# A layer-norm pipeline staggered by half tiles, w1 in column quarters, and segment sums moved from TensorE to VectorE

## The chip, the cores and the metric

The kernel runs on one core of one Trainium2 chip. The time is device microseconds (us) of that core for one execution. A difference of under 2% in either direction is called "same", with a 95% interval beside it.

Engine names in the profile: PE is the TensorE matmul, PEld its weight load, DVE is VectorE, ACT is ScalarE, POOL is GpSimd, SP is SyncE, which here only issues DMAs. "SPq" is SyncE's own queue of DMA issues. L401 is line 401 of the kernel that the profile belongs to, so the same statement has another number in another kernel.

## The reference, cut to what matters

```python
x  = A_x                                   # 2048 tokens x 1024, bf16
xn = layernorm(x)
return x + A(xn, mem0, Wq, Wk, Wv, Wo) + B(xn, w1, w2, w3, w4)

def B(x, w1, w2, w3, w4):
    h  = gelu(layernorm(x) @ w1)           # 1024 -> 1024
    hs = shift_four_column_groups(h) @ w2  # tokens moved by +1, -1, +2, -2
    x1 = x + hs
    return x1 + gelu(layernorm(x1) @ w3) @ w4     # 1024 -> 3584 -> 1024

def A(x, mem, ...):                        # 64 segments of 32 tokens, 8 memory tokens
    for s in range(64):                    # 32 heads of 128
        h = concat(mem, x[segment s])
        o = attention(h) @ Wo              # memory tokens see all 40, the others none later than themselves
        mem = o[:8]; outs.append(o[8:])
```

The kernel runs B first and fits work for A between its matmuls. The part of A that matters here starts from the sums of `xn` over each segment of 32 tokens. They are multiplied by Wv ("vb" units: 32 matmuls each), then by Wo ("g" units), then by Wv again ("vr" units), to get values for the memory tokens before the attention begins. There are eight units of each kind, in that order.

## The kernel before

Comments in the code are added here. The order of stages is: stage 1 (layer-norms, transposes, w1, gelu), stage 2 (w2, residual, second layer-norm), four passes of 512 tokens each through w3 and then w4, the V stage, the attention, and the output projection. A tile is 128 tokens. `NPE` is the number of tiles that are normalised on VectorE and transposed by TensorE; the later ones are normalised on ScalarE and transposed by DMA.

```python
NPE = 8
load_x(0)
load_x(1)
for c in range(2):                                       # w1 in two column halves
    nc.sync.dma_start(w1_sb[:, :, c * 512:(c + 1) * 512], w1_v[:, :, c * 512:(c + 1) * 512])
    load_x(c + 2)
# ... cut
def norm2(n, xn2T, jj):
    if n < NPE:
        nc.vector.tensor_scalar(xn2[:], xts[n][:], mv[:, 0:1], rr[:, 1:2], op0=ALU.subtract, op1=ALU.mult)
    else:
        nc.scalar.activation(xn2[:], xts[n][:], ACTF.Identity, bias=nm2[:], scale=rr[:, 1:2])
        nc.sync.dma_start_transpose(xn2T[:, jj], xn2[:])

def seg_sums(n, xn):                                     # in stage 1, from SBUF
    ps = psum0.tile([P, KT, 4], F32, tag="xs")
    for k in range(KT):
        nc.tensor.matmul(ps[:, k, :], xn[:, k * P:(k + 1) * P], segsum[:], start=True, stop=True)
    nc.scalar.copy(xsum[:, :, 4 * n:4 * n + 4], ps[:])
# ... cut: stage 1 and stage 2
for _ in range(4):
    load_w3()
for c in range(7):                                       # w4, 7 x 1 MB, on the SP queue
    nc.sync.dma_start(w4_sb[:, 4 * c:4 * (c + 1), :], w4_v[:, 4 * c:4 * (c + 1), :])

def unit_vb(hg):
    wv = wtile()
    nc.gpsimd.dma_start(wv[:], Wv_v[:, :, hg * 512:(hg + 1) * 512])
    def run():
        ps = psum3.tile([P, 4, NQ], F32, tag="vr")       # NQ = 71 columns
        for hh in range(4):
            for k in range(KT):
                nc.tensor.matmul(ps[:, hh, :], wv[:, k, hh * P:(hh + 1) * P], xb[:, k, :NQ], start=(k == 0), stop=(k == KT - 1))
        # ... cut
def load_r1(n):                                          # the residual of tile n, two buffers
    nc.sync.dma_start(r1s[n][0][:], R1_v[:, n, :])
    nc.sync.dma_start(r1s[n][1][:], x_v[:, n, :])

load_r1(0)
for tb in range(4):                                      # the four passes
    depth = 1 if tb < 2 else 2
    for f in range(FT):                                  # w3, FT = 28
        # ... cut: 8 matmuls and a gelu
        if tb == 0 and f == 20:
            mem_start()                                  # copies xsum and the memory's sum to xb
        if tb > 0 and f % 7 == 6:
            spec_step(depth)                             # runs one vb, g or vr unit, loads the next
    if tb == 0:
        spec_load()
    for j in range(4):                                   # w4, one tile at a time
        n = tb * 4 + j
        R1, xt = r1s.pop(n)
        load_r1(n + 1)
        nc.gpsimd.tensor_tensor(R1[:], R1[:], xt[:], op=ALU.add)
        # ... cut: 2 x 28 matmuls, two adds to R1 on VectorE
        if n == NT - 1:
            while pending or units:
                spec_step(depth)
        elif n > 0:
            spec_step(depth)
```

Of the kernel before, what the change touches and what calls it, by code (L numbers as in the profile page):

```python
# [77 lines left out]
def kernel(  # L78
# [47 lines left out]
    segsum_np = np.zeros((P, 4), np.float32)  # L126
    for t in range(P):
        segsum_np[t, t // SEG] = 1.0
    segsum = const_tile("c_segsum", segsum_np)
# [54 lines left out]
    with tc.manual_schedule(engines={mybir.EngineType.PE, mybir.EngineType.SP, mybir.EngineType.Pool}), ExitStack() as actx:  # L184
# [6 lines left out]
        with ExitStack() as bctx:  # L191
            w3ctx = bctx.enter_context(ExitStack())
            xctx = bctx.enter_context(ExitStack())
            xsum = xctx.enter_context(tc.tile_pool(name="xs", bufs=1)).tile([P, KT, NSEG], BF16)
# [12 lines left out]
            with ExitStack() as hctx:  # L207
# [7 lines left out]
                with ExitStack() as p0:  # L215
# [3 lines left out]
                    NPE = 8  # L219
# [9 lines left out]
                    load_x(1)  # L229
                    for c in range(2):  # L230
                        nc.sync.dma_start(w1_sb[:, :, c * 512:(c + 1) * 512], w1_v[:, :, c * 512:(c + 1) * 512])
                        load_x(c + 2)
                    for n in range(4, 7):
                        load_x(n)
# [54 lines left out]
                    def seg_sums(n, xn):  # L289
                        ps = psum0.tile([P, KT, 4], F32, tag="xs")  # L290
                        for k in range(KT):
                            nc.tensor.matmul(ps[:, k, :], xn[:, k * P:(k + 1) * P], segsum[:], start=True, stop=True)  # L292
                        nc.scalar.copy(xsum[:, :, 4 * n:4 * n + 4], ps[:])

                    def stage1(n0, nt, xn2T, between):
                        w = nt * P
                        for co in range(KT):
                            ps = psum.tile([P, 512], F32, tag="mm", bufs=4)
                            for k in range(KT):
                                nc.tensor.matmul(ps[:, :w].rearrange("p (n t) -> p n t", t=P), w1_sb[:, k, co * P:(co + 1) * P],  # L300
                                                 xn2T[:, :nt, k, :], start=(k == 0), stop=(k == KT - 1))
                            nc.scalar.activation(hTB[:, co, 2 + n0 * P:2 + n0 * P + w], ps[:, :w], ACTF.Gelu_apprx_tanh)
                            for f in between.get(co, ()):
                                f()
# [11 lines left out]
                    for i in range(13):  # L316
                        nc.tensor.matmul(ps[:], wz[:, :P], wz[:], start=(i == 0), stop=(i == 12))
                    norm_stats(0)
                    norm_stats(1, 0)
                    t0 = xn2T_tile()  # L320
                    xn2 = norm2(0, t0, 0)
                    transposes(xn2, t0, 0, 0)
                    transposes(xn2, t0, 0, 1, on_dve=True)
# [3 lines left out]
                    t1 = xn2T_tile()  # L327
                    xn2 = norm2(1, t1, 0)
                    norm_stats(2)

                    def first(xn2=xn2, t1=t1):
                        transposes(xn2, t1, 0, 0)
                        transposes(xn2, t1, 0, 1)
                    xns = {}

                    def sums_of(n):
                        if n in xns:
                            seg_sums(n, xns.pop(n))

                    stage1(0, 1, t0, {3: [first], 4: [lambda: norm_stats(3)]})  # L340
                    groups = [(1, 1)] + [(n, 2) for n in range(2, NT, 2)]
                    tiles2 = {1: t1}
                    xn2s = {}

                    def prep(n):
                        xn2s[n] = norm2(n, tiles2[n - n % 2], n % 2)
                        norm_stats(n + 2)
                        done = range(n - 2, n - 1) if n < NPE else range(NPE - 2, n + 1) if n == NPE else range(n, n + 1)
                        for m in done:
                            xns[m] = norm1(m)  # L350

                    def tr(n, half):
                        transposes(xn2s[n], tiles2[n - n % 2], n % 2, half)


                    for gi, (n0, nt) in enumerate(groups):
                        between = {c: [] for c in range(KT)}
                        if gi + 1 < len(groups) and groups[gi + 1][0] < NPE:
                            m0 = groups[gi + 1][0]
                            tiles2[m0] = xn2T_tile()  # L360
                            prep(m0)
                            between[1] += [lambda m0=m0: tr(m0, 0), lambda m0=m0: prep(m0 + 1)]
                            between[2] += [lambda m0=m0: tr(m0, 1)]
                            between[5] += [lambda m0=m0: tr(m0 + 1, 0)]
                            between[6] += [lambda m0=m0: tr(m0 + 1, 1)]
                        if gi + 2 < len(groups) and groups[gi + 2][0] >= NPE:
                            m0 = groups[gi + 2][0]
                            tiles2[m0] = xn2T_tile()
                            between[2] += [lambda m0=m0: prep(m0)]
                            between[5] += [lambda m0=m0: prep(m0 + 1)]  # L370
                        between[3] += [lambda n0=n0: sums_of(n0 - 1)]
                        between[4] += [lambda n0=n0: sums_of(n0 - 2)]
                        stage1(n0, nt, tiles2[n0], between)
                    for n in range(NT):
                        sums_of(n)
# [29 lines left out]
            with ExitStack() as p3:  # L405
# [5 lines left out]
                m0 = ring.tile([M, D], BF16, tag="m0", bufs=1)  # L411
                nc.sync.dma_start(m0[:], A_mem0[0])
# [5 lines left out]
                vbT = big.tile([P, H, NQ + 1], BF16)  # L418
                xb = big.tile([P, KT, NQ + 1], BF16)
                gps = []  # L420

                def mem_start():
# [4 lines left out]
                    t0 = ring.tile([P, KT, 1], F32, tag="t0", bufs=1)  # L427
                    nc.vector.tensor_tensor(t0[:], ps9[:, :, M:M + 1], xsum[:, :, 0:1], op=ALU.add)
                    nc.vector.tensor_copy(xb[:, :, 8:NQ], xsum[:, :, 1:NSEG])
                    nc.vector.tensor_copy(xb[:, :, 0:8], t0[:].to_broadcast((P, KT, 8)))  # L430

                def unit_vb(hg):
# [3 lines left out]
                    def run():  # L436
                        ps = psum3.tile([P, 4, NQ], F32, tag="vr")
                        for hh in range(4):
                            for k in range(KT):
                                nc.tensor.matmul(ps[:, hh, :], wv[:, k, hh * P:(hh + 1) * P], xb[:, k, :NQ], start=(k == 0), stop=(k == KT - 1))  # L440
                        nc.vector.tensor_scalar(vbT[:, hg * 4:(hg + 1) * 4, :NQ], ps[:], 1.0 / L, None, op0=ALU.mult)
                    return run

                def unit_g(c):
# [3 lines left out]
                    def run():  # L448
                        if c == 0:
                            gps.extend(psum3.tile([P, 4, NQ], F32, tag="g", name=f"gps{i}") for i in range(2))  # L450
                        for hh in range(4):
                            h = c * 4 + hh
                            for k in range(KT):
                                nc.tensor.matmul(gps[k // 4][:, k % 4, :], wo[:, hh, k * P:(k + 1) * P], vbT[:, h, :NQ],  # L454
# [542 lines left out]
```

## Time and profile before

| | before |
|---|---|
| median of the first 3 runs | 1529.47 us (1528.92 to 1529.94) |
| span of the profiled run | 1527.2 us |
| PE busy | 1512.6 us, 99% |
| all waits of PE together | 5.7 us |
| first w1 matmul; stage 2 begins | 9.55 us; 75.09 us |
| first vb unit begins | 203.04 us |

These lines are from the page of the kernel before: the busy time of each engine (share of the span, number of instructions), and the chain of work that ended last, by engine.

```profile
PE 1512.6 (99%) x9810; PEld 810.3 (53%) x9883; DVE 530.1 (35%) x1131; ACT 506.8 (33%) x1155; POOL 178.8 (12%) x248
...
PE 98%; DMA 1%; DVE 0%; issue 0%; ACT 0%; SPq 0%
```

The next lines are PE's waits in the kernel before: what it could not start, what it waited for, and the total in us, the count, and the longest.

```profile
PE ps L300 <- DMA w_sb<-in_B_w_dram: 2.0, 1, 2.0
PE ps L283 <- DVE xn L264: 1.3, 1, 1.3
PE warm L317 <- DVE wz L311: 1.3, 1, 1.3
PE ps L292 <- DVE xnk L273: 0.7, 1, 0.7
PE ps L300 <- ACT xn2T L287: 0.2, 1, 0.2
PE pso L710 <- issue: 0.2, 1, 0.2
```

TensorE bounds this kernel. Every wait that it has lies in the first 20 us, but for 0.4 us. A change can gain only by taking work from TensorE, by shortening that start, or by shortening the 5.1 us between the last matmul and the end.

### The profile page before, as it was taken

What the parts mean: (1) busy time and instruction counts of PE and PEld (TensorE: products, weight loads), DVE (VectorE), ACT (ScalarE), POOL (GpSimd) and SP (SyncE); (2) the same over time, 40 slices, a digit from 0 to 9 for tenths busy, and PEclk for the clock granted to TensorE, in tenths of its full rate; (3) what the DMA queues carried; (4) which work ended last, traced back from release to release, by engine and by line L of the source; (5) the groups of instructions that cost most, each with busy time, mean ns of one, the idle gap of its engine ahead of it and who ended that gap; (6) DMA issues with size and microseconds to landing.
All of it is one profiled execution on the core that took longest, in us unless ns stands there. A gap on an engine that the chain in (4) does not pass through costs nothing.

```text
span 1527.2 us, 24314 instructions
## 1 busy us (share of the span) xinstructions
PE 1512.6 (99%) x9810; PEld 810.3 (53%) x9883; DVE 530.1 (35%) x1131; ACT 506.8 (33%) x1155; POOL 178.8 (12%) x248
## 2 busy tenths in 40 slices
PE   8999999999999999999999999999999999999998
PEld 7844444444444444444466645654665555445554
DVE  8284010000210122211146624650664266426641
ACT  5533202103012011111156614650663266326620
POOL 5232020221211222100000010001000100010001
PEclk9999999999999999999999999999999999999999
DMA  8679543452352877632399947992997389728611
GB/s 252 186 221 308 208 158 118 142 183 90 115 176 80 213 259 255 223 123 82 125 242 247 235 133 183 234 244 74 229 251 187 106 222 227 183 80 203 177 46 51
DMA packets 287373, 270.03 MB, mean 177 GB/s; under 512 B 136875, under 2 KB 255040, under 8 KB 287000
## 3 DMA queue, kind: packets, MB, share of 16 engines
q1 hardware_dynamic: 265208, 185.79, 47.5%
q0 software_dynamic: 22048, 82.63, 15.5%
q8 instruction: 80, 1.31, 0.4%
q14 instruction: 37, 0.30, 0.1%
HBM read 190.98 MB, written 46.19 MB: 155 GB/s over the span
## 4 chain that ended last, share of the span: by engine, by line
PE 98%; DMA 1%; DVE 0%; issue 0%; ACT 0%; SPq 0%
PE ps L652 30%; PE ps L579 14%; PE pso L710 14%; PE ps L523 13%; PE ps L548 13%; PE ps L387 4%; PE ps L300 3%; PE psS L667 2%; PE psO L691 2%; DMA xt<-in_A_x_dram 1%; PE ps L474 1%; PE ps L837 1%; PE ps L440 1%; PE gps L454 1%; PE ps L292 0%
## 5 line engine op out<-in xcount | busy, mean ns | idle before, releaser
L652 PE MATMUL ps<-hTb,wt 128*128 128x396 bf16 (+3 forms) x2560 | 509.5, 343 | 0.0
L652 PEld LDWEIGHTS <-wt 128*128 128x128 bf16 x2560 | 234.2, 98 | 166.1
L710 PE MATMUL pso<-wo_sb,oX 128*128 128x512 bf16 x1001 | 223.4, 379 | 1.3 <-issue 0.2
L579 PE MATMUL ps<-wt,xT 128*128 128x512 bf16 x1004 | 220.1, 379 | 1.1
L523 PE MATMUL ps<-xn3T,w_sb 128*128 128x512 bf16 x896 | 195.7, 379 | 0.0
L548 PE MATMUL ps<-w_sb,h3T 128*128 128x512 bf16 x872 | 194.3, 379 | 1.2
L579 PEld LDWEIGHTS <-xT 128*128 128x128 bf16 x1024 | 100.2, 98 | 120.8
L524 ACT ACTIVATE h3T<-ps 128x512 bf16<-128x512 f32 x112 | 66.9, 597 | 292.1 <-PE ps L523 291.2
L710 PEld LDWEIGHTS <-oX 128*128 128x128 bf16 x1024 | 98.8, 98 | 115.3
L658 ACT CAST KT<-ps 128x396 bf16<-128x396 f32 (+3 forms) x160 | 82.3, 514 | 224.0 <-PE ps L652 222.5
L548 PEld LDWEIGHTS <-h3T 128*128 128x128 bf16 x896 | 86.8, 98 | 102.8
L523 PEld LDWEIGHTS <-w_sb 128*128 128x128 bf16 x896 | 86.8, 98 | 102.7
L673 DVE TENSOR_REDUCE sums<-sm 99x4 f32<-99x396 f32 (+2 forms) x176 | 97.6, 555 | 113.4 <-ACT sm L671 113.4
L669 DVE TENSOR_TENSOR sm<-psS,c_mask_reg_sb 99x396 f32<-99x396 f32 x160 | 91.3, 571 | 90.2 <-PE psS L667 89.7
L671 ACT ACTIVATE sm<-sm 99x396 f32<-99x396 f32 (+2 forms) x176 | 92.8, 527 | 71.6 <-DVE sm L669 70.9
L581 ACT CAST Vs<-ps 128x512 bf16<-128x512 f32 x64 | 37.4, 586 | 233.3 <-PE ps L579 169.2
L660 ACT ACTIVATE QT<-ps 128x396 bf16<-128x396 f32 (+3 forms) x160 | 84.2, 526 | 74.0 <-PE ps L652 54.1
L585 DVE CAST Vs<-ps 128x512 bf16<-128x512 f32 x64 | 44.3, 692 | 170.0 <-PE ps L579 157.1
L549 DVE TENSOR_TENSOR R<-ps,R 128x512 f32<-128x512 f32 x32 | 22.1, 692 | 232.0 <-PE ps L548 221.1
L679 DVE TENSOR_TENSOR Pn<-sm,rs 99x396 bf16<-99x396 f32 (+2 forms) x176 | 98.9, 562 | 6.3 <-DVE rs L675 0.5
L692 ACT CAST oX<-psO 128x384 bf16<-128x384 f32 (+1 forms) x176 | 82.4, 468 | 8.3 <-PE psO L691 7.8
L717 POOL DMA_DIRECT2D out_dram<-ot x30 | 16.4, 546 | 583.5 <-DVE ot L716 577.6
(118 smaller groups left out, 978.3 us busy)
## 6 DMA issues: line engine op xcount, KB each, us to landing
wt<-in_A_Wk_dram SPq DMA_DIRECT2D x78, 512.0 KB
wt<-in_A_Wq_dram SPq DMA_DIRECT2D x76, 512.0 KB
wt<-in_A_Wv_dram POOLq DMA_DIRECT2D x24, 1024.0 KB, 6.8
V_scratch<-Vs SPq DMA_DIRECT2D x32, 512.0 KB
V<-V_scratch SPq DMA_DIRECT2D x32, 384.0 KB
w_sb<-in_B_w_dram SPq DMA_DIRECT2D x9, 1024.0 KB
R_scratch<-x POOLq DMA_DIRECT2D x16, 512.0 KB, 3.9
R<-R_scratch SPq DMA_DIRECT2D x16, 512.0 KB
```

What stands on the lines that cost most here:

```text
L523: nc.tensor.matmul(ps[:].rearrange("p (n t) -> p n t", t=P), w3_sb[:, k, f * P:(f + 1) * P], xn3T[tb][:, :, k, :], start=(k == 0), stop=(k ...
L548: nc.tensor.matmul(ps[:], h3T[:, f, j * P:(j + 1) * P], w4_sb[:, f, ch * 512:(ch + 1) * 512], start=(f == 0), stop=(f == FT - 1))
L579: nc.tensor.matmul(ps[:], xT[:, m4 * 4 + j, k, :], wv[:, k, :], start=(k == 0), stop=(k == KT - 1))
L652: nc.tensor.matmul(ps[:, :nb] if flat else ps[:, :nb].rearrange("p (t c) -> p t c", t=nt), w[:, k, hh * P:(hh + 1) * P], B["rhs"](k), star ...
L658: nc.scalar.copy(o, i)
L660: nc.scalar.mul(o, i, scale)
L669: nc.vector.tensor_tensor(sm[:T, :, :T], S3, t["mask"][:].unsqueeze(1).to_broadcast((T, 4, T)), op=ALU.add)
L671: nc.scalar.activation(e[:T, :, :T], sm[:T, :, :T], ACTF.Exp, scale=LN2)
L673: nc.vector.tensor_reduce(ss, e[:T, :, :T], axis=AX.X, op=ALU.add)
L679: nc.vector.tensor_tensor(Pn[:T, :, :T], e[:T, :, :T], rs[:T, :].unsqueeze(2).to_broadcast((T, 4, T)), op=ALU.mult)
L692: nc.scalar.copy(oX[:, hs_, at:at + nt], O3[:, :, 0:nt])
L710: nc.tensor.matmul(self.ps[:], self.oX[:, h, self.gl * P:(self.gl + 1) * P], wo_sb[:, h, self.cc], start=(h == 0), stop=(h == H - 1))
```

## The change

The intent has three parts.

1. The front end. w1 arrives in four column quarters, so the first matmul can start earlier. The first four tiles run singly. The statistics of the first half of tile n+1 stand in VectorE's queue ahead of the normalisation of tile n. `NPE` falls from 8 to 6, so tiles 6 and 7 are normalised on ScalarE.
2. The segment sums leave TensorE. Each tile of `xn` is read back from DRAM by a transposing DMA, in the first w3 pass, and VectorE reduces it. The vb and g units work on 64 columns, not 71, and `mem_start` moves behind the first tile of the first w4 pass.
3. The tail. The last output block is split into two of 256 columns.

Two small edits ride along and are cut from the diff below: TensorE runs 15 warm-up matmuls before the first tile, not 13, and the tile of the memory tokens is loaded later, just before the first w3 pass.

The diff, cut to its core:

```diff
-                    NPE = 8
+                    NPE = 6
                     load_x(0)
-                    load_x(1)
-                    for c in range(2):
-                        nc.sync.dma_start(w1_sb[:, :, c * 512:(c + 1) * 512], w1_v[:, :, c * 512:(c + 1) * 512])
-                        load_x(c + 2)
-                    for n in range(4, 7):
+                    for c in range(4):
+                        nc.sync.dma_start(w1_sb[:, :, c * 256:(c + 1) * 256], w1_v[:, :, c * 256:(c + 1) * 256])
+                        if c < 2:
+                            load_x(c + 1)
+                    for n in range(3, 7):
                         load_x(n)
 ... (cut: the PE seg_sums of stage 1 and its calls are removed; warm-up, helpers and the old loop over the tiles)
+                    for n in range(1, NPE):
+                        norm_stats(n + 1, 0)
+                        norm2_of(n)
+                        norm_stats(n + 1, 1)
+                        if n > 1:
+                            norm1(n - 2)
+                        if n < 4:
+                            stage1(n - 1, 1, tiles2[(n - 1) // 2 * 2], {5: [lambda n=n: tr(n, 0)], 6: [lambda n=n: tr(n, 1)]}, (n - 1) % 2)
+                    prep6 = {2: [lambda: norm_stats(7), lambda: norm2_of(6), lambda: norm1(NPE - 2)],
+                             5: [lambda: norm_stats(8), lambda: norm2_of(7), lambda: norm1(NPE - 1)]}
+                    for h in range(2):
+                        for c in range(2):
+                            prep6.setdefault(4 + 2 * h + c, []).append(lambda h=h, c=c: tr(4 + h, c))
+                    stage1(3, 1, tiles2[2], prep6, 1)
 ... (cut)
+                def seg_sums(n):
+                    xr = ring.tile([P, KT, P], BF16, tag="xr")
+                    nc.sync.dma_start_transpose(xr[:], xn_v[:, n, :])
+                    with nc.allow_low_precision(reason="sums are accumulated in fp32 and rounded once"):
+                        nc.vector.tensor_reduce(xb[:, :, 4 * n:4 * n + 4], xr[:].rearrange("p k (s t) -> p k s t", t=SEG), axis=AX.X, op=ALU.add)
 ... (cut: 71 columns become 64 in the vb and g units)
-                        if tb == 0 and f == 20:
-                            mem_start()
+                        if tb == 0 and 2 <= f < NT + 2:
+                            seg_sums(f - 2)
 ... (cut)
                         elif n > 0:
                             spec_step(depth)
+                        else:
+                            mem_start()
 ... (cut: the last output block in two halves)
```

## The prediction

> **What bounds it.** TensorE. The page gives PE 1512.6 us busy of a 1527.2 us span (99%), and the chain of waits is PE for 98%. PE's waits add up to only 5.7 us: 1.3 for the zero tile, 1.3 for the first normalised tile, 2.0 for w1, 0.7 for a segment sum, 0.4 others. Windows by microsecond show a further loss: the granted clock is 0.50 from 10.9 to 14.3 us, after PE sat idle for w1. [...] The change can gain only in removed PE work, the first 30 us and the last 5.
>
> **PE work removed, all on the chain.**
> - Segment sums: 16 groups of 8 small matmuls, 0.21 us each (next start minus start): -3.3 us, plus the 0.7 us wait.
> - Transposes by PE for 6 tiles, not 8: 4 groups of 4 at 0.22 us: -0.9.
> - Two more token tiles run singly: 128 columns cost 56 ns, 256 cost 109: +0.2.
> - 512 matmuls of 71 columns become 64: 32 take 1.04 us now, 32.5 ns each; estimate 29.5: -1.5.
> - Tail: the last add (0.69 us) and store shrink to 256 columns: -0.4.
>
> **PE waits moved.** w1 in quarters lets the first token tile start at about 7.9, not 9.5. But a quarter has 512 B rows: the trace's packets take 84 ns at 2048 B, 46 at 1024, so about 27 at 512 (estimate), twice as many for the same bytes. [...] So the last quarter and x3, which stand behind it, land no earlier than before (x3: 13.6), I estimate 14 and 14.7. VectorE now has bn_stats of tile n+1 before the normalisation of tile n, so x3 holds up tile 2.
>
> From there VectorE needs 2.8 us a tile, TensorE about 4.1. I walked the queues in program order with these durations; for the kernel before this gives stage 1 ending at 74.9, where the trace has 75.0. For the changed kernel it shows a **new wait**: tile 6 is normalised on ScalarE, and that stands in ScalarE's queue inside the fourth tile's matmuls, before the copies of the transposes of tiles 4 and 5. Its statistics are not ready until about 27, so ScalarE blocks, and PE waits 2 to 2.5 us for transpose buffers, then 1.3, then 0.7. Some 4 us of the PE work saved is given back, and the clock may halve once more (up to 1.7 us). Stage 1 then ends at 73 to 77, against 75.0.
>
> **Segment sums on VectorE** (about 1.1 us each) and their DMA transposes fall in the first w3 pass, where VectorE is idle: free.
>
> **Sum.** Stage 1: about 0 (-2 to +2); narrower matmuls -1.5; tail -0.4. **1527.3 us, range 1523.5 to 1531.3.** Chances: faster by over 2% 0.01, within 2% 0.985, slower by over 2% 0.005.
>
> **What would show it.** Segment-sum matmuls gone from PE; first w1 matmul near 8; no 0.50 clock at 11 to 14; a ScalarE wait for the tile-6 bias near 25 to 27, followed by PE waits for xn2T/transposes of tile 5; stage 2 starting at 73 to 77; the w2 to last phases unchanged, about 1.5 us shorter in the vb and g units.
>
> **What would make it wrong.** 512 B packets as fast per byte as 1024 B ones (then 1524), or limited by packet count (w1 complete only at 17 to 22: 1530 to 1535); late transposes holding VectorE in the w4 pass.

The sum (stage 1 about 0, narrower matmuls -1.5, tail -0.4) comes to 1527.3 us. The "up to 1.7 us" for one more halving of the clock is the author's estimate, half of the 3.4 us at 0.50 in the trace of the kernel before; that an idle PE would bring it again was an assumption from that one case.

## More of the kernel before

One timeline of PE in the kernel before is needed later: start, duration, line, operation, and a bracket with the idle time if there was any. L548 is w4, L440 is a vb unit.

```profile
178.86 24.34 PE L548 MATMUL ps<-w_sb,h3T 128*128 128x512 bf16 x109
203.04 1.20 PE L440 MATMUL ps<-xb,wt 128*128 128x71 bf16 x32
204.07 12.25 PE L548 MATMUL ps<-w_sb,h3T 128*128 128x512 bf16 x55
216.16 1.20 PE L440 MATMUL ps<-xb,wt 128*128 128x71 bf16 x32
```

There is no bracket: the vb units run without a wait, because `mem_start` had filled their input `xb` from 166.5 us on, in the first w3 pass, out of sums that stage 1 had left.

## The result, and the profile after

The kernel after takes 1541.75 us in the median of four runs (1539.80 to 1545.55), against 1529.35 (1528.92 to 1529.94) for four runs of the kernel before. The ratio is 1.0084, with a 95% interval of 1.0064 to 1.0104. Ratios in this document are the mean time of one kernel's runs over that of the other's runs of the same rounds, so they are not quite the ratio of the medians that are quoted. The change is a loss of 0.8%; the prediction was a gain of 0.1%, and the time lies 10 us above the top of its range.

The profile belongs to the slowest of the four runs (1545.55 us, span 1543.6). These are its page lines, the same two as before.

```profile
PE 1513.4 (98%) x9765; PEld 810.8 (53%) x9837; DVE 547.2 (35%) x1146; ACT 506.9 (33%) x1145; POOL 179.4 (12%) x250
...
PE 91%; DMA 4%; SPq 2%; DVE 2%; issue 1%; ACT 0%; POOL 0%; DVEq 0%; POOLq 0%
```

PE has fewer instructions and yet no less busy time, and it is no longer 98% of the chain that ended last: DMA, SyncE's queue and VectorE have come into it. The starts of the stages, read from the first matmul of each, tell where (us):

| | before | after | after minus before |
|---|---|---|---|
| first w1 matmul | 9.55 | 8.23 | -1.3 |
| stage 2 | 75.09 | 74.00 | -1.1 |
| first w3 pass | 130.13 | 129.25 | -0.9 |
| first w4 pass | 178.86 | 177.60 | -1.3 |
| first vb unit | 203.04 | 215.87 | **+12.8** |
| second w3 pass | 230.33 | 245.36 | +15.0 |
| V stage | 542.57 | 556.21 | +13.6 |
| attention | 763.58 | 777.23 | +13.7 |
| last matmul ends | 1522.12 | 1539.37 | +17.3 |
| span | 1527.21 | 1543.56 | +16.4 |

The whole loss, and more, appears between the first w4 pass and the second w3 pass. These are PE's waits in the kernel after.

```profile
PE ps L418 <- DVE xb L401: 13.5, 1, 13.5
PE ps L277 <- ACT xn2T L281: 3.0, 2, 1.8
PE psO L673 <- DMA PT<-Pn: 2.0, 1, 2.0
PE ps L288 <- DMA w_sb<-in_B_w_dram: 1.4, 2, 1.0
...
PE ps L288 <- ACT xn2T L281: 0.5, 1, 0.5
```

The first line is new and is as large as the loss: a vb unit (L418) waited 13.5 us for the segment sums (L401). PE's timeline of the kernel after shows it in place.

```profile
190.06 12.26 PE L529 MATMUL ps<-w_sb,h3T 128*128 128x512 bf16 x55
215.87 1.86 PE L418 MATMUL ps<-xb,wt 128*128 128x64 bf16 x32 [13.54 <-DVE xb L401]
217.95 13.62 PE L529 MATMUL ps<-w_sb,h3T 128*128 128x512 bf16 x54 [0.22 <-issue]
231.41 1.10 PE L418 MATMUL ps<-xb,wt 128*128 128x64 bf16 x32
```

The unit after the wait took 1.86 us and the next one 1.10; the w4 group took 13.62, where it takes 12.25 in the kernel before. The windows of the kernel after say why. The columns are the window, its length, then busy us and instructions of PE, PEld, DVE, ACT, POOL, then the granted PE clock, the DMA share and GB/s.

```profile
202.00:208.00 6.00, 0.33 (x2) 0.04 (x1) 3.97 (x6) 0.00 (x0) 0.60 (x1) 0.96 0.71 178
208.00:216.00 8.00, 0.13 (x4) 0.13 (x4) 4.17 (x4) 0.00 (x0) 0.00 (x0) 0.50 0.74 158
216.00:222.00 6.00, 5.78 (x44) 3.23 (x44) 1.36 (x3) 0.00 (x0) 3.00 (x2) 0.57 0.47 188
```

PE ran out of work at 202.3 us. The clock was halved (0.50) 5.2 us later, and it came back only 5.3 us after the work did: the half clock lasts from 207.5 to 221.2 us, 13.7 us. From the start of the first vb unit to that of the second, 15.54 us pass; from the second to the third it is 13.02 (231.41 to 244.43). The half clock and its surroundings so cost 2.5 us on top of the 13.5.

Why were the sums late? These are the reduces on VectorE's timeline in the kernel after, and VectorE's total wait for them.

```profile
170.93 2.35 DVE L401 TENSOR_REDUCE xb<-xr 128x32 bf16<-128x1024 bf16 x2 [39.55 <-DMA xr<-xn_scratch]
...
180.50 1.22 DVE L401 TENSOR_REDUCE xb<-xr 128x32 bf16<-128x1024 bf16 x1 [2.46 <-DMA xr<-xn_scratch]
191.42 1.22 DVE L401 TENSOR_REDUCE xb<-xr 128x32 bf16<-128x1024 bf16 x1 [9.69 <-DMA xr<-xn_scratch]
...
214.59 1.22 DVE L401 TENSOR_REDUCE xb<-xr 128x32 bf16<-128x1024 bf16 x1 [1.65 <-DMA xr<-xn_scratch]
```

```profile
DVE xb L401 <- DMA xr<-xn_scratch: 63.7, 14, 39.6
```

A reduce takes 1.22 us, so the 16 of them take 19.5 us. VectorE had that time to spare. It stood idle for 63.7 us in front of them, waiting for data. The first sum began at 170.9, only 7 us before the first w3 pass ended; the last ended at 215.8, where TensorE needed it at 202.3. SyncE's queue in the kernel after shows what stood ahead of the transposes (L390 is w4, L399 the transposes).

```profile
138.45 16.91 SPq L390 DMA_DIRECT2D w_sb<-in_B_w_dram  x7
...
159.05 53.36 SPq L399 DMA_TRANSPOSE xr<-xn_scratch  x16
212.46 0.58 SPq L493 DMA_DIRECT2D R<-R_scratch  x1
```

The 7 MB of w4 are issued first, from 138.5 to 155.4. The transposes are issued from 159.05, and the last only at 212.4. The critical chain of the kernel after (start, duration, what) measures one step of them.

```profile
159.05 11.46 DMA xr<-xn_scratch
...
170.93 1.25 DVE xb L401 x2
172.18 3.48 DMA xr<-xn_scratch
...
178.26 13.13 DMA xr<-xn_scratch
...
201.83 0.02 issue
201.85 3.25 DMA xr<-xn_scratch
205.10 0.02 issue
205.13 1.22 DVE xb L401
```

Three things are to be seen here.

- The first transpose took 11.5 us, behind w4. In the packets of the trace the 2 KB ones, of the loads issued before it, run on until about 168 us (the last ends at 169.1), and the 256 B packets of the transposes begin at 167.4, 8.4 us after the first transpose was issued.
- In the steady state a transpose takes 3.3 to 3.5 us from a free buffer to landing. With two buffers, and each held by a reduce of 1.22 us as well, a pair takes about 4.7 us: 2.3 us a tile, 37 us for 16.
- One transpose took 13.1 us. In that time the first load of Wv (1 MB, issued by GpSimd at 178.06) was on its way; it took 13.3 us, where the median of these loads is 7.1. That the one slowed the other is a guess at this point, which e8 tests.

In the front end the picture is as predicted. These are PE's transposes of tiles 4 and 5 in the kernel after:

```profile
28.18 0.38 PE L277 MATMUL ps<-c_ident_sb,xn 128*128 128x128 bf16 x4 [1.81 <-ACT xn2T L281]
...
30.18 0.58 PE L277 MATMUL ps<-c_ident_sb,xn 128*128 128x128 bf16 x4 [1.17 <-ACT xn2T L281]
```

And this is ScalarE just before them, normalising tile 6:

```profile
26.09 1.24 ACT L260 ACTIVATE xn<-xt,nm,rr 128x1024 bf16<-128x1024 bf16 x1 [1.63 <-POOL nm L252]
```

ScalarE blocks for 1.63 us on the statistics of tile 6, and the copies that free PE's transpose buffers stand behind it in program order. In the trace the first of them runs at 27.55 us, after the normalisation (26.09, 1.24 us), and PE waits 1.81 us for it.

At the far end, one wait of 2.0 us for `PT<-Pn` near 819 us in the attention, and 3.4 us at half clock after it, from 821.9 to 825.3 us (about 1.7 us lost, an estimate: half of that stretch), make up the 3.6 us by which the attention and the output take longer than before. The kernel before has no such wait.

### The profile page after: what moved, and what is told of

It is laid out like the page before. It is cut to its first block, busy times and chain, and to the rows that moved or that the text cites. A ratio compares the mean times of both kernels' runs of the same rounds, so it can differ in the third digit from the quotient of the medians.

```text
span 1543.6 us, 24268 instructions
## 1 busy us (share of the span) xinstructions
PE 1513.4 (98%) x9765; PEld 810.8 (53%) x9837; DVE 547.2 (35%) x1146; ACT 506.9 (33%) x1145; POOL 179.4 (12%) x250
## 3 DMA queue, kind: packets, MB, share of 16 engines
q0 software_dynamic: 22032, 82.63, 16.1%
## 4 chain that ended last, share of the span: by engine, by line
PE 91%; DMA 4%; SPq 2%; DVE 2%; issue 1%; ACT 0%; POOL 0%; DVEq 0%; POOLq 0%
PE ps L634 30%; PE pso L692 14%; PE ps L561 14%; PE ps L529 11%; PE ps L504 9%; PE ps L363 4%; DMA xr<-xn_scratch 3%; PE ps L288 3%; PE psS L649 2%; PE psO L673 2%; SPq L390 1%; DVE xb L401 1%; PE ps L453 1%; PE ps L418 1%; PE ps L821 1%
## 5 line engine op out<-in xcount | busy, mean ns | idle before, releaser
L692 PE MATMUL pso<-wo_sb,oX 128*128 128x512 bf16 (+1 forms) x1034 | 223.6, 372 | 1.2 <-issue 0.2
L692 PEld LDWEIGHTS <-oX 128*128 128x128 bf16 x1056 | 101.9, 98 | 112.5
L699 POOL DMA_DIRECT2D out_dram<-ot x30 | 16.3, 545 | 586.8 <-DVE ot L698 580.9
```

What stands on the lines that cost most here:

```text
L692: nc.tensor.matmul(self.ps[:, :self.w], self.oX[:, h, self.gl * P:(self.gl + 1) * P], wo_sb[:, h, self.cc], start=(h == 0), stop=(h == H - 1))
```

## The experiments

All thirteen kernels gave correct results, and all runs but the single one of `e8_wv_behind_sums` (state unknown) were in the fast state. The sets e1 to e4, e5 to e8, e9 to e12 and e13 ran on four different chips, so between sets the ratios to the kernel before are compared, not the medians. The times of the kernel before in the same rounds were 1530.91 us (median of 7) for e1 to e4, 1529.90 (9) for e5 to e8, 1530.44 (11) for e9 to e12, and 1531.14 (11) for e13. The theory at the start was that the late segment sums cost the time; the rivals were that the new front end costs it, or that sums and w4 are merely in the wrong order on the queue.

The start of stage 2 is the measure of the front end, and the start of the V stage that of everything up to the last w4 pass:

| kernel | median us | ratio (95% interval) | stage 2 | first vb | V stage |
|---|---|---|---|---|---|
| before | 1529.35 | | 75.09 | 203.04 | 542.57 |
| after | 1541.75 | 1.0084 (1.0064 to 1.0104) | 74.00 | 215.87 | 556.21 |
| e1_front_only | 1531.11 | 1.0002 (0.9986 to 1.0019) | 77.45 | 205.61 | 543.43 |
| e2_sums_only | 1540.62 | 1.0061 (1.0043 to 1.0079) | 74.48 | 215.18 | 554.93 |
| e3_vb_later | 1551.76 | 1.0148 (1.0128 to 1.0168) | 73.27 | 227.34 | 540.99 |
| e4_norm6_later | 1549.26 | 1.0119 (1.0102 to 1.0136) | 74.95 | 233.06 | 546.71 |
| e5_vb_later_made_up | 1527.83 | 0.9987 (0.9972 to 1.0003) | 74.15 | 226.48 | 540.13 |
| e6_sums_between_w4 | 1541.02 | 1.0071 (1.0056 to 1.0087) | 72.93 | 216.09 | 553.91 |
| e7_both_mended | 1537.71 | 1.0052 (1.0038 to 1.0065) | 70.74 | 214.84 | 552.67 |
| e8_wv_behind_sums | 1537.91 (one run) | | 73.63 | 208.94 | 548.45 |
| e9_later_and_eight | 1531.40 | 1.0003 (0.9988 to 1.0017) | 70.19 | 225.80 | 539.46 |
| e10_halves | 1531.04 | 1.0000 (0.9986 to 1.0015) | 71.32 | 231.83 | 545.49 |
| e11_pe_sums_eight | 1527.35 | 0.9982 (0.9967 to 0.9996) | 73.81 | 201.97 | 539.79 |
| e12_two_dmas_fewer | 1535.37 | 1.0036 (1.0021 to 1.0051) | 70.05 | 227.68 | 541.33 |
| e13_residual_first | 1524.18 | 0.9958 (0.9945 to 0.9970) | 70.36 | 222.70 | 536.35 |

The start of stage 2 scatters from trace to trace. Five kernels with the same front end (after, e3, e5, e6, e8) show 72.93 to 74.15, and four with eight tiles (e7, e9, e12, e13) show 70.05 to 70.74. A difference of about 1 us from one trace each is therefore an indication and no more. Part of the scatter is the clock: the first five all have the waits of 1.8 and 1.2 us near 28 and 30 us, but a half-clock window follows them only in after and e5 (74.00 and 74.15), not in e3, e6 and e8 (72.93 to 73.63).

### e1_front_only: the change without part 2

The kernel after, with the segment sums back on TensorE in stage 1. The 64 columns stay.

```diff
+                    def seg_sums(n, xn):
+                        ps = psum0.tile([P, KT, 4], F32, tag="xs")
+                        for k in range(KT):
+                            nc.tensor.matmul(ps[:, k, :], xn[:, k * P:(k + 1) * P], segsum[:], start=True, stop=True)
+                        nc.scalar.copy(xsum[:, :, 4 * n:4 * n + 4], ps[:])
 ... (cut: called in stage 1; mem_start copies xsum to xb)
-                        if tb == 0 and 2 <= f < NT + 2:
-                            seg_sums(f - 2)
```

> The changed kernel with its segment sums back on TensorE (16 groups of 8 small matmuls in stage 1); everything else as changed, the 64-column vb and g units too. Theory: the loss comes from the segment sums on VectorE, which come too late for the first vb unit. Then the 13.5 us wait of the first vb matmuls is gone, stage 2 starts at about 77 us (74.0 plus 16 x 0.21), and the time is 1529 +- 2 us. Rival: the loss comes from the new front end (NPE 6, quarters of w1) and shows up later; then the time stays above 1536.

The loss is gone: 1531.11 us, ratio 1.0002 (0.1 us above the expected range; the kernel before took 1530.91 in the same rounds). No wait for `xb` is left, and stage 2 begins at 77.45, 3.45 us later than in the kernel after. So the sums on VectorE do take 3.45 us off stage 1, and they are also where the loss comes from. The front end on its own loses time: stage 2 begins 2.4 us later than in the kernel before. The narrower units bring that down to 0.9 us at the V stage, and the tail is 0.9 us shorter.

### e2_sums_only: part 2 on the kernel before

The mirror image: the old front end, with the sums on VectorE and the 64 columns as in the change. The edit is the part of the change's diff from `seg_sums` on.

```diff
-                    def seg_sums(n, xn):          # on TensorE, in stage 1, with its calls
 ... (cut)
+                def seg_sums(n):                  # as in the change
+                    xr = ring.tile([P, KT, P], BF16, tag="xr")
+                    nc.sync.dma_start_transpose(xr[:], xn_v[:, n, :])
 ... (cut)
+                        if tb == 0 and 2 <= f < NT + 2:
+                            seg_sums(f - 2)
```

> The kernel before with only the segment sums moved to VectorE (and the 64 columns that go with it). Theory: this part alone brings the wait of 12 to 14 us in the first vb unit and a half-clock window behind it; stage 2 starts near 71.5 us (3.5 earlier than before), so the time is 1537 to 1541. Rival (front end to blame): about 1524.

The loss is there without the new front end: 1540.62 us, ratio 1.0061. This is PE's wait in this kernel:

```profile
PE ps L420 <- DVE xb L403: 12.4, 1, 12.4
```

Together with e1 this settles which part of the change is to blame. A miss is the start of stage 2, 74.48, where about 71.5 was expected. With the sums gone from the old front end TensorE meets more waits there: 2.1 us for DMA-transposed tiles (none in the kernel before), 2.4 for w1 (2.0) and 1.9 for VectorE (1.3). The old front end was bound by its pipeline and not only by TensorE's work.

### e3_vb_later: the first unit waits for a later slot

The kernel after, in which the first w4 pass runs a unit only after its last tile. TensorE no longer asks for the sums at 202 us.

```diff
-                        elif n > 0:
+                        elif n > 2:
                             spec_step(depth)
-                        else:
+                        elif n == 0:
                             mem_start()
```

> The changed kernel with the first vb unit three slots later: it runs after token tile 3 of the w4 pass, not after tile 1 (one line). Nothing about the transposes or the sums changes. Theory: only the wait of the vb unit for xb costs time; it disappears, with its clock window, and the time is 1541.7 - 13.5 - 1.5 = about 1526.5 (1525 to 1528.5). Rival: the 16 transposes delay the w4 pass in other ways too (residual tiles queued behind them, DMA share), so PE waits elsewhere in the pass and the time stays above 1532.

This was a clear miss: 1551.76 us, ratio 1.0148. The wait for the sums was gone, and the V stage began at 540.99, 15.2 us earlier than in the kernel after. Then the time went again. PE and ScalarE in this kernel:

```profile
PE ps L561 <- ACT Vs L563: 16.2, 1, 16.2
```

```profile
563.60 1.07 ACT L563 CAST Vs<-ps 128x512 bf16<-128x512 f32 x2 [75.29 <-DMA Vmem_scratch<-vrt]
```

The units form a chain of 24 through the passes. With two slots taken out, the last vr unit ran two slots later, and its store to DRAM was issued at 561.37 us, behind transposes on SyncE's queue. The V stage needs that store, and TensorE waited 16.2 us for it. The theory survives and the remedy was incomplete: a unit that is moved must be made up for before the end of the chain. The rival was right in a small part: TensorE also waited 1.6 us at 215 us for a residual sum on VectorE, a wait that e9 comes back to.

### e4_norm6_later: tiles 6 and 7 normalised behind the copies

On top of e3, the normalisations of tiles 6 and 7 on ScalarE move behind the copies of tiles 4 and 5.

```diff
-                    prep6 = {2: [lambda: norm_stats(7), lambda: norm2_of(6), lambda: norm1(NPE - 2)],
-                             5: [lambda: norm_stats(8), lambda: norm2_of(7), lambda: norm1(NPE - 1)]}
+                    prep6 = {2: [lambda: norm_stats(7), lambda: norm1(NPE - 2)], 5: [lambda: norm_stats(8), lambda: norm1(NPE - 1)]}
 ... (cut)
+                    prep6[7] += [lambda: norm2_of(6), lambda: norm2_of(7)]
```

> The kernel of the run above, and tiles 6 and 7 normalised on ScalarE after the copies of the transposes of tiles 4 and 5, not before them. Theory from the walk of the queues: the PE waits of 1.8, 1.2 and 0.5 us at 26 to 31 us and the half-clock window after them (about 1.7 us) go, stage 2 starts at 69 to 70.5 instead of 74.0, and the time is 4 to 5 us under the run above (about 1522). Rival: ScalarE is not the cause but VectorE's pace is; then the waits move by less than 1 us.

A miss too. The two waits of PE for ScalarE's copies (3.0 us) are gone, as expected. A wait of 3.6 us for tile 6's DMA transpose took their place, and stage 2 began at 74.95, later than in e3. The wait at the start of the V stage was there again, 14.1 us, hence the time of 1549.26. In this order the normalisation on ScalarE is late for the DMA transpose behind it, so this change of order is no cure.

### e5_vb_later_made_up: e3 with the two slots made up

```diff
-                        if tb > 0 and f % 7 == 6:
+                        if tb > 0 and f % 7 == 6 or tb == 2 and f in (10, 24):
                             spec_step(depth)
```

> The run with the first vb unit three slots later turned the wait into one of 16 us at the start of the V stage: the vr units ended two slots later, and their DMAs stood behind the transposes of x on the same queue. Here the units start as late, but two extra slots in the third w3 pass let the vr units end where they did. Theory: the vb wait is the loss and the 16 us came from the late vr units; both are gone, and the time is 1525 to 1528. Rival: the V stage waits because of the slower DMA queue in general; then it waits again, and the time stays above 1535.

1527.83 us, ratio 0.9987: as expected, and with neither the wait for the sums nor that of the V stage. These are PE's two longest waits in this kernel:

```profile
PE ps L277 <- ACT xn2T L281: 3.0, 2, 1.8
PE psO L673 <- DMA PT<-Pn: 1.6, 1, 1.6
```

The V stage begins at 540.13, 16.1 us earlier than in the kernel after. This shows the cause of the loss. The sums ended at 209.0 us, sooner than the 215.8 of the kernel after but still too late for the slot at 202.3; nobody asked for them there. The prediction's own figure (1527.3) is about what the change gives once the sums have the time that they need.

### e6_sums_between_w4: the transposes among w4's loads

This is the rival: the transposes were late because of w4. Two or three transposes now follow each of the seven w4 loads.

```diff
-                for c in range(7):
-                    nc.sync.dma_start(w4_sb[:, 4 * c:4 * (c + 1), :], w4_v[:, 4 * c:4 * (c + 1), :])
 ... (cut)
+                for c in range(7):
+                    nc.sync.dma_start(w4_sb[:, 4 * c:4 * (c + 1), :], w4_v[:, 4 * c:4 * (c + 1), :])
+                    for n in ((0, 1), (2, 3), (4, 5), (6, 7, 8), (9, 10, 11), (12, 13), (14, 15))[c]:
+                        seg_sums(n)
```

> The changed kernel with its 16 transposes put between the seven w4 loads on the same queue (two or three after each), not behind them all. Same DMAs, same sums, same units. Theory: the sums are late because their transposes stand behind 7 MB of w4; here the last sum is done by about 180 us, before PE is ready for the vb unit at 202, the 13.5 us wait and the clock window go, and the time is 1526 to 1528 (unless the last w4 block lands after 178, then up to 5 us more, seen as PE waits for w4). Rival: the transposes are slow in themselves (2.4 us each whatever stands ahead, 8 us more beside the Wv load): then w4 is late by what the sums gain, and the time stays above 1535.

1541.02 us, ratio 1.0071: no gain over the kernel after. PE's wait in this kernel:

```profile
PE ps L529 <- DMA w_sb<-in_B_w_dram: 11.1, 2, 6.1
```

The sums came in time (the last ended at 197.3, where about 180 was expected), and w4 came late by about as much as had been gained. SyncE stood in the transposes, each waiting for one of two buffers, and could not issue the w4 load behind it: the last w4 load was issued at 186.9 us, where the first w4 matmul came at 176.5. So it is not only the order. In this trace the two or three transposes between one w4 load and the next held SyncE for 2.8 to 10.9 us, and the loads behind them on its queue came that much later.

### e7_both_mended: e6 with NPE 8

Tiles 6 and 7 are again normalised on VectorE and transposed by TensorE, inside the matmuls of tiles 4 and 5.

```diff
-                    NPE = 6
+                    NPE = 8
 ... (cut)
+                        if n0 == 4:
+                            for h in range(2):
+                                for c in range(2):
+                                    between[1 + 2 * h + c].append(lambda h=h, c=c: tr(6 + h, c))
                         if n0 + 4 < NT:
-                            between[2] += [lambda n0=n0: prep(n0 + 4)]
-                            between[5] += [lambda n0=n0: prep(n0 + 5)]
+                            c0, c1 = (5, 7) if n0 == 4 else (2, 5)
+                            between[c0] += [lambda n0=n0: prep(n0 + 4)]
+                            between[c1] += [lambda n0=n0: prep(n0 + 5)]
```

> The run above, and eight tiles (not six) normalised on VectorE and transposed by TensorE, so that ScalarE's first own normalisation comes two tiles later. Theory: the PE waits at 26 to 31 us (3.5 us) and the half-clock window after them go, 0.9 us of transposes comes back: stage 2 starts at 70 to 71 instead of 74, and the time is 3 to 4 us below the run above, about 1523, faster than both kernels. Rival: VectorE's pace holds the tiles back; stage 2 starts at 73 or later.

Stage 2 began at 70.74 us, 2.2 us earlier than in e6 and within what the theory of the front end expected. The waits of 1.8 and 1.2 us for ScalarE's copies were gone. The wait for w4 was now 13.4 us, so the time was still 1537.71, where about 1523 was expected.

### e8_wv_behind_sums: the first Wv load behind the transposes

```diff
-                    nc.gpsimd.dma_start(wv[:], Wv_v[:, :, hg * 512:(hg + 1) * 512])
+                    (nc.gpsimd if hg else nc.sync).dma_start(wv[:], Wv_v[:, :, hg * 512:(hg + 1) * 512])
```

> The changed kernel with the first Wv load (1 MB) issued on the same queue as the 16 transposes, behind them, so that none of its packets flow beside them. A probe, not an improvement. Theory: the hole of 8 us in the row of sums (182 to 191 us) is this load; without it the last sum ends near 207 instead of 215.8, and the vb unit then waits for Wv, to 213 to 220. Rival: the hole has another cause and stays.

The hole was gone (the longest gap between two sums was 2.5 us, not 9.7), and the last sum ended at 205.8 us, 10 us earlier. This one run points to the Wv load but does not settle it. In e5 the load runs beside the transposes just as in the kernel after, and there it took 6.7 us, not 13.3, and the longest gap was 2.5 us as well. In the other traces with sums behind w4 and the load beside them the gap is 4.2 to 9.7 us, mostly longer where the load takes longer; why they slow each other in some runs and not in others is open. In e8 TensorE waited all the same, for the Wv load itself, until 208.9 (213 to 220 was expected):

```profile
PE ps L418 <- DMA wt<-in_A_Wv_dram: 7.0, 1, 7.0
```

Even undisturbed, the sums end 3.5 us after 202.3, when TensorE first needs them. Only a later demand or an earlier supply can help.

### e9_later_and_eight: e5 with NPE 8

```diff
-                    NPE = 6
+                    NPE = 8
 ... (cut: on e5, with the same edits as in e7)
```

> Both mends that worked: the first vb unit three slots later with two slots made up, and eight tiles normalised on VectorE and transposed by TensorE. Theory: the two losses are separate and add up; stage 2 starts at 70.7 as in the run with eight tiles (74.2 in the run with the later unit alone) and no wait for xb, so the time is 1527.8 - 3.4 = about 1524.5 (1523 to 1526), ahead of the kernel before by some 5 us. Rival: they interfere (an earlier stage 2 moves the pass against the DMA queue) and a new wait over 2 us appears between 130 and 560 us.

Stage 2 began at 70.19 us, 4.9 us earlier than in the kernel before, as the theory had it. The time did not follow: 1531.40 us in the median of six, between 1526.10 and 1533.08, ratio 1.0003. PE and GpSimd in this kernel (the profiled run is the fastest, 1526.10):

```profile
PE ps L534 <- DVE R L535: 3.1, 1, 3.1
```

```profile
210.84 2.11 POOL L530 TENSOR_TENSOR R<-R,xr 128x1024 f32<-128x1024 f32 x1 [13.54 <-DMA xr<-in_A_x_dram]
```

This was the rival's expectation. The loads of tile 1's residual stand behind the 16 transposes on SyncE's queue and were issued at 205 to 207 us. GpSimd waited 13.5 us for them, VectorE, which adds w4's PSUM buffers to GpSimd's sum, waited 3.8 us for that sum, and TensorE waited 3.1 us. It is not the early stage 2 alone that brings this wait: e4, whose stage 2 begins at 74.95, has one of 4.0. What it follows, in the six traces with the later vb unit and the residual behind the transposes, is the time from the first w4 matmul to the issue of the last transpose: 26.7 us in e5 (no wait), 28.9 in e3 (1.6), 30.0 in e9 (3.1), 30.7 in e12 (3.4), 31.5 in e4 (4.0) and 32.8 in e10 (5.6).

### e10_halves: e9 with w1 in two halves

```diff
-                    for c in range(4):
-                        nc.sync.dma_start(w1_sb[:, :, c * 256:(c + 1) * 256], w1_v[:, :, c * 256:(c + 1) * 256])
-                        if c < 2:
-                            load_x(c + 1)
-                    for n in range(3, 7):
+                    load_x(1)
+                    for c in range(2):
+                        nc.sync.dma_start(w1_sb[:, :, c * 512:(c + 1) * 512], w1_v[:, :, c * 512:(c + 1) * 512])
+                        load_x(c + 2)
+                    for n in range(4, 7):
                         load_x(n)
```

> The run above with w1 in two column halves and x1 ahead of it, as the kernel before loads it. Theory A: quarters are worth the earlier start of the first tile only; with halves the first w1 matmul stands at 9.5 instead of 8.2, PE waits 2.2 and 1.6 us for w1, and (with a half-clock window near 11 to 14 as before) stage 2 starts at 71.5 to 72.2, 1 to 1.5 us later. Against it, Theory B: the wait of about 2 us of one output matmul for a probability transpose near 800 us comes with the count of DMAs on the one queue (semaphores go round in eight; here the count is again the same modulo eight as in the kernel before, which has no such wait). If B holds, that wait is absent here and the time is within 1.5 us of the run above; if not, it is there and the time is 1 to 1.5 us longer.

Stage 2 began at 71.32 us, 0.6 to 1.3 us later than in the four traces with quarters and eight tiles (70.05 to 70.74): that is what the quarters are worth in this pipeline, as far as single traces tell. Two details were a miss: the first w1 matmul came at 8.55, not 9.5, and no half-clock window followed. The total, 1531.04, does not tell halves from quarters, because the wait for the residual was 5.6 us here. Theory B fell: the wait for `PT<-Pn` was there, 3.9 us in four places.

### e11_pe_sums_eight: e1 with NPE 8

```diff
-                    NPE = 6
+                    NPE = 8
 ... (cut: on e1, with the same edits as in e7)
```

> The new front with eight tiles and the segment sums left on TensorE (units at their old slots). It tells what moving the sums is worth once nothing waits for them. Theory: 16 x 0.21 us on the chain: stage 2 starts at about 74 and the time is 3 to 3.5 us above the first run of this set, about 1528. Rival: the small matmuls fill waits of stage 1 that would be there anyway, and the difference is under 1.5 us.

1527.35 us, ratio 0.9982. Stage 2 began at 73.81, 3.6 us after that of e9: the price of 16 segment sums on TensorE. The time was not 3 to 3.5 us above e9's, as expected, but 4 us below it, because of e9's own waits. In exchange nothing had to be ready by a deadline, and the four runs agree within 1.4 us.

### e12_two_dmas_fewer: e9 with w2 in two loads

This was to explain the small wait for `PT<-Pn` in the attention, which every kernel with the new front end has (1.4 to 3.9 us) and neither the kernel before nor e2 has. The theory was that the semaphores by which DMAs report their end matter here. In the traces the DMAs of SyncE's queue take eight of them strictly in turn (all 597 DMAs in the kernel before and all 618 in the kernel after), so by the theory two DMAs fewer would put the attention's transposes back in step.

```diff
-                    for i in range(4):
-                        nc.sync.dma_start(w2_sb[:, 2 * i:2 * i + 2, :], w2_v[:, 2 * i:2 * i + 2, :])
+                    for i in range(2):
+                        nc.sync.dma_start(w2_sb[:, 4 * i:4 * i + 4, :], w2_v[:, 4 * i:4 * i + 4, :])
```

> The first run of this set with w2 in two DMAs instead of four, the same bytes. The only purpose: the count of DMAs on the queue is then, modulo eight, that of the kernel before. Theory B (round of eight semaphores): the wait of an output matmul for its probability transpose near 800 us (1.4 to 2.4 us in every kernel with the new front, absent in the kernel before and in the run with the sums alone) disappears, and the time falls by 1.5 to 3 us. Rival: it stays, so its cause is another.

The theory fell here too: the wait stayed (3.3 us in three places). The time was 1535.37. The cause of this wait stays open.

### e13_residual_first: e9 with the residual ahead of the transposes

```diff
                 def load_r1(n):
-                    if n < NT:
+                    if n < NT and n not in r1s:
 ... (cut)
                 load_r1(0)
+                load_r1(1)
```

> The kernel with the later vb unit and eight tiles, and the residual tiles of the second token tile loaded ahead of the 16 transposes on the queue, not behind them. Theory: the wait of 3.1 us (5.6 and 3.4 in its two sisters) of the w4 pass for the residual sum on VectorE is the second debt of the transposes: the queue is in order, and the residuals stand behind them (GpSimd waited 13.5 us for that tile). With them first, that wait is gone, and the gain of the eight tiles holds: 1524 to 1526.5, and the spread between runs (1526 to 1533 there) narrows. Rival: the wait only moves to the third token tile, whose residuals can be asked for no earlier, because two buffers serve them; then the wait stays above 2 us and the time stays near 1530.

1524.18 us in the median of six (1523.04 to 1527.64), ratio 0.9958, interval 0.9945 to 0.9970. It beats both kernels: the one before by 0.4%, and the one after by about 1.2% (ratios 0.9958 and 1.0084, from different rounds). PE's waits in this kernel:

```profile
PE psO L679 <- DMA PT<-Pn: 2.7, 2, 1.5
PE ps L288 <- DMA w_sb<-in_B_w_dram: 1.5, 2, 1.0
PE warm L305 <- DVE wz L299: 1.3, 1, 1.3
PE ps L288 <- ACT xn2T L281: 0.5, 1, 0.5
PE pso L698 <- issue: 0.2, 1, 0.2
```

The wait for the residual is gone, and between 165 and 245 us PE is busy for 79.73 us of 80 at a clock of 1.00. Two edited lines, which change the order on the queue, turned e9's ratio of 1.0003 into this. The last transpose was issued 33.1 us after the first w4 matmul, later than in the six traces listed under e9, and yet there was no wait. As e5 showed the first cause, the sums' deadline, so this shows the second, the load that the transposes held up. The gain over the kernel before, in the profiled runs, is 4.7 us at stage 2 and 6.2 at the V stage; 2.8 us of it are then given back in the attention, where the wait for `PT<-Pn` is 2.7, and the tail returns 1.3.

### What stays open

Why the attention waits for `PT<-Pn` in the kernels with the new front end isn't known. The time of e9 varied by 7 us from run to run, and only its fastest run was traced. More than two buffers for the transposes were not tried. Why the row of sums had a hole of 9.7 us in the kernel after and none in e5 isn't known either. The profiled run of the kernel after is 3.8 us slower than the median of its runs, so the sizes of its waits in a typical run may be smaller than those shown.

## Why the prediction was wrong

Predicted were 1527.3 us, and 1523.5 to 1531.3; measured were 1541.75. The class (within 2%) was right. Point by point:

- **What bounds it** (TensorE, 98% of the chain): right, and e13 shows it, where removed work and removed waits became time.
- **Segment sums on TensorE, -3.3 us and -0.7 of wait**: right in size in the new front end. Stage 2 begins 3.45 us earlier in the kernel after than in e1, and 3.6 earlier in e9 than in e11. On the old front end (e2) the same removal gained only 0.6.
- **w1 in quarters**: start at 8.23, predicted 7.9. 512 B packets took 27 ns, as estimated. x3 landed at 13.6, where 14.7 was estimated. The half clock that stood from 10.8 to 14.2 us in the kernel before is gone, as predicted. e10 puts the worth of the quarters at about 1 us.
- **The new wait behind tile 6 on ScalarE**: right in place and cause. Predicted 2 to 2.5, 1.3 and 0.7 us; measured 1.8, 1.2 and 0.5. The clock was halved once more, from 30.0 to 33.4, as said. That part was partly luck: with the same waits it was not halved in e3, e6 and e8. With NPE 8 the waits and the half clock vanish (e7, e9).
- **Stage 2 at 73 to 77**: 74.00. The 1.1 us to the kernel before lie within the scatter between traces of this front end (72.93 to 74.15).
- **Narrower matmuls, -1.5**: right. 32 of them take 0.93 us, not 1.03, and the lag behind the kernel before falls from 15.0 us at the second w3 pass to 13.6 at the V stage.
- **The tail, -0.4**: somewhat more. From the last matmul to the end 4.19 us pass, not 5.09.
- **The step that failed**: "Segment sums on VectorE (about 1.1 us each) and their DMA transposes fall in the first w3 pass, where VectorE is idle: free." The engine time was nearly right, 1.22 us each, and VectorE was idle. What was wrong is that they fall in the first w3 pass. Program order placed them there. Their data came when SyncE's queue and the DMA engines delivered it, and of the 16 reduces only four had begun when the first w4 matmul started (177.6). The step counted what the moved work costs the engine that it moved to. It did not ask when its input arrives, nor when its result is due. Cost of this one term: 13.5 us of wait and 2.5 us of half clock, against 0.
- **"The w2 to last phases unchanged"**: wrong for the same reason, and for the 3.6 us in the attention (`PT<-Pn` and its half clock), which nothing in the prediction covered and which stay unexplained.
- **"Late transposes holding VectorE in the w4 pass"** stood among what would make the prediction wrong. This was near: the transposes were late. It was TensorE's own vb unit that they held, not VectorE's other work, and the range was not widened for it.

The sum of the terms in the profiled runs: -1.1 (stage 1) + 13.5 + 2.5 (sums) - 1.3 (narrower units, with what else lies before the V stage) + 3.6 (attention) - 0.9 (tail) = 16.3 us, where the spans differ by 16.4.

The warning was there in the kernel before. Its timeline shows the first vb unit at 203.04 us without a wait, and its SyncE queue already issued 7 MB of w4 in the same pass. Sixteen transposes of 256 KB behind them, with two buffers, had a deadline that could have been worked out.

## What to carry to other kernels

Work that moves to an idle engine is free only if its input arrives and its result is due at times that fit; here it cost 13.5 us of wait and 2.5 us of half clock. For each moved piece write down when its data is issued, what stands ahead of it on the same DMA queue, how many buffers it cycles through, and when the first consumer on the bounding engine asks. In these traces DMAs that waited for a buffer also held up the later ones on SyncE's queue (in e6 w4, whose last load was issued 10.4 us after the first w4 matmul; in e9 the residual, for which GpSimd waited 13.5 us), so put short urgent loads ahead of a long buffered train, as e13 did (ratio 0.9958, against 1.0003 for e9).

## What these traces measured of the clock, the transposes and the queue

- **Half clock after short idle times.** Three stretches of half clock lasted 3.4 us each: 30.0 to 33.4 and 821.9 to 825.3 (kernel after), and 10.8 to 14.2 (kernel before). In the 3.4 us just before them PE was partly busy: 0.83, 1.39 and 1.36 us, and the longest gaps in those times were 1.8 to 2.0 us. Two times of the same length with 1.60 us busy (25.9 to 29.3, e3) and 1.62 (200.7 to 204.1, kernel after) were not followed at once by half clock. The busy times are those of the profile, whose matmul ends are modelled. Five cases do not show a rule.
- **DMA transposes.** One of a 256 KB tile from DRAM took 3.3 to 3.5 us from a free buffer to landing (kernel after), and two buffers gave one tile per 2.3 us, about 110 GB/s by these two figures. More in flight was not tried.
- **DMAs of two issuers.** In the kernel after one transpose took 13.1 us and one 1 MB load 13.3 us, beside each other, where other transposes took 3.3 to 3.5 and the median load 7.1; in e5 the same load in the same place took 6.7.
- **A queue held by waits for buffers.** The 16 transposes held SyncE's queue for 53 us in the kernel after, and in e9, where they held it for 50, two short loads of a residual behind them cost TensorE 3.1 us.
